# One TensorE visit for the values of a head pair's three tiles, in a fused windowed attention and feed-forward kernel

## The chip, the cores and the metric

The kernel runs on one core of one Trainium2 chip. The metric is the device time of one execution in microseconds. Engines are named as in the profile: PE is TensorE's matmul stream and PEld its weight loads, DVE is VectorE, ACT is ScalarE, POOL is GpSimd, SP is the engine that issues the DMAs (SPq its queue).

## The reference

Attention over 4 batches of 8 heads, 768 positions and 64 columns a head, in which a position sees the 4 first keys (sinks) and the last 128; its output, 3072 tokens of 512 columns, goes through a feed-forward of width 2048 with an ELU.

```python
scores = scale * np.matmul(q, k.transpose(0, 1, 3, 2))
rel = pos[:, None] - pos[None, :]
keep = (pos[None, :] < n_sink) | ((rel >= 0) & (rel < window))
scores = np.where(keep, scores, -1000000000.0)
a = np.exp(scores - np.max(scores, axis=-1, keepdims=True))
a = a / (np.sum(a, axis=-1, keepdims=True) + 1e-09)
x = np.matmul(a, v)   # then (B, S, H * D), as 3072 tokens of 512
h = x @ w_in
g = np.where(h > 0.0, h, np.exp(np.minimum(h, 0.0)) - 1.0)
out = g @ w_out
```

## The kernel before

The 3072 tokens are 24 tiles of 128, six to a batch, grouped into nine chunks (`SIZES`, L42): chunks 0 to 2 have two tiles, chunks 3 to 8 three. Each chunk goes through attention, head pair by head pair (four pairs of two heads), and then through the feed-forward, in 16 blocks of 128 hidden columns. The feed-forward of chunks 0 and 1 is cut in halves (`PARTS`), since the weights arrive and are converted meanwhile.

For a tile of a head pair, attention is a chain over all engines. TensorE makes the scores of the two heads (L560 and L561 for each head; L567 in the first two chunks) into two score banks. DVE masks them and takes the maximum (L586), ACT takes the exponential (L588), ACT and DVE make the reciprocal of the sum (L592, L593), ACT and DVE write the probabilities in a high and a low fp16 half into a buffer pq (L600, L601), POOL writes the sinks (L607 to L611), and SP issues a transposing DMA from pq to a buffer pt (L619). Then TensorE multiplies pt with the values (`values`, L622 to L635): 6 matmuls for the first tile of a batch, 12 for the second, 14 for the others. These three parts of po (one PSUM bank, `po=1` in `RINGS`) become the pair's x by ACT L643 and DVE L644. Keys come in as kqs and are split into a high part (ACT L503) and a low part (POOL L507, L509).

In the feed-forward an h block is 12 matmuls of a block's input weights with the x of the four pairs (`stage1`, L671); two h banks take turns. ACT L679, DVE L681 and L682 and ACT L684 with POOL L685 make the ELU in two halves; an acc block (`stage2`, L692) multiplies these with the output weights into one bank for each tile. A weight's conversion is ACT L287, DVE L288, L289 and L290, ACT L436, POOL L437, 32 times, all of it within the start-up.

The order on every engine is decided ahead of time by a planner (`Plan`, L94). Each step is a task with an engine, a cost in us, and the tasks that it needs. TensorE's tasks carry a place `pos`; they form lines (1 scores, 2 values, 0 the rest) whose own order is fixed by it. `forward` goes through the tasks as if they ran, and takes on TensorE the line head that is ready and has the earliest place; the other engines take the ready task with the earliest due time. It does this in 8 rounds and keeps the best. `keep_order` (L774) then emits the instructions in that order. A task on TensorE is emitted in one piece; waits are set for each instruction by the buffers that it reads and writes.

Before, each tile's values are a task of their own (L637), with a place that is the same for the tiles of a pair but for 0.01 a tile.

Of the kernel before, what the change touches and what calls it, by code (L numbers as in the profile page):

```python
# [44 lines left out]
PARTS = [(0, 0, HALF), (1, 0, HALF), (0, HALF, NF), (1, HALF, NF)] + [(c, 0, NF) for c in range(2, len(SIZES))]  # L45
LAG = 2
ROUNDS = 8
WHOLE = 2
DUP = 2
AHEAD = 5  # L50
V_AT = 7
V_AT0 = 5.0
# [41 lines left out]
class Plan:  # L94
# [7 lines left out]
    def add(self, eng, dur, fn, *args, deps=(), lat=0.0, pos=None, or_=None, line=0):  # L102

        t = Task(eng, dur, fn, args, deps, lat, pos)
        t.line = line
        if or_:
            t.ways[or_[0]] = or_[1:]
        self.tasks.append(t)
        return t

    def ring(self, name, writers, users):

        r = self.rings.setdefault(name, [])
        r.append((writers, users))
# [229 lines left out]
def fast_path(tc, ctx, first, kq, vx, wt, out, nw, flag):  # L344
# [44 lines left out]
    add, ring = plan.add, plan.ring  # L389
# [54 lines left out]
    base, pos = {}, 0  # L444
# [27 lines left out]
    def attention(c):  # L472
        ts = CHUNKS[c]
        nt, kts = len(ts), key_tiles(ts)
# [5 lines left out]
        if c == 0:  # L480
            at = [-3.0 - V_AT0 - 3.0 + 1.2 * (k - n) for k in range(n)]
        elif c == 1:
            at = [-1.0 + k * (base[c] - 1.0 - V_AT) / (n - 1) for k in range(n)]
        else:
            at = [base[c] - 2.0 - V_AT - (n - 1 - k) * (base[c] - base[c - 1]) / n for k in range(n)]
# [32 lines left out]
        k = 0  # L518
        for p in range(NP):
# [10 lines left out]
            va = add("ACT", act_us(vw, True), lambda vraw=vraw, vhi=vhi: nc.scalar.activation(vhi, vraw, AF.Copy, scale=V_SCALE), deps=[ld])  # L530
            vb = add("DVE", dve_us(vw) + 0.1, lambda vraw=vraw, vhi=vhi, vlo=vlo: nc.vector.scalar_tensor_tensor(vlo, vraw, V_SCALE, vhi, ALU.mult, ALU.subtract), deps=[va])
            v_users = []
            ring("vs", [ld or va], [va, vb])
            if far:

                vb = add("ACT", 0.3, lambda vhi=vhi, vlo=vlo: nc.scalar.activation(vhi[64:72, nk * P :], vlo[64:72, nk * P :], AF.Copy), deps=[vb])
            ring("vhl", [va], v_users)

            po = po_ps[slot("po")]
            vals = []  # L540
            for g in ts:
                t, j = g % NT, ts.index(g)
                nb = 1 if t == 0 else 2
# [90 lines left out]
                            vo = nk * P + e * D  # L634
                            nc.tensor.matmul(po[e * D : (e + 1) * D, oc], vhi[:, vo : vo + D], pt[:, 8, :], start=False, stop=end)  # L635

                val = add("PE", 0.17 * nb + (0.05 if t >= 2 else 0.0) + (0.2 if j == 0 else 0.0), values, deps=[tr, va, vb], pos=at[k - j + nt - 1] + (V_AT0 if c == 0 else V_AT) + 0.01 * j, line=2)  # L637
                ring("pt", [tr], [val])
                vals.append(val)
                v_users.append(val)  # L640
                k += 1
            xh, xl = x_room(qc)
            fa = add("ACT", act_us(qc, True), lambda xh=xh, po=po: nc.scalar.activation(xh, po[:, :qc], AF.Copy, scale=PO_SCALE), deps=[vals[-1]])  # L643
            fb = add("DVE", dve_us(qc) + 0.1, lambda xh=xh, xl=xl, po=po: nc.vector.scalar_tensor_tensor(xl, po[:, :qc], PO_SCALE, xh, ALU.mult, ALU.subtract), deps=[fa])  # L644
# [372 lines left out]
```

## Time and profile before

| | us |
|---|---|
| runs | 657.74, 660.30, 660.76 (median 660.3) |
| the profiled execution | 658.03 |
| its span, first to last instruction | 656.2 |
| busy: TensorE, DVE, ACT, POOL | 611.0, 458.4, 456.3, 338.8 |

The profile is of one execution. A line of its tables names the source line, the engine, the operation, and what is written from what. Busy times are sums over an engine's instructions with overlaps counted once, so the durations of an engine's rows can add up to more. Ends of matmuls are modelled: durations of neighbouring PE rows overlap, and what a block takes is read from start to start.

### The profile page before, as it was taken

How to read it: one execution, taken by the hardware profiler on the slowest of the kernel's cores; microseconds unless marked ns; L12 is line 12 of the kernel's file. 1: busy time of each engine (PE TensorE's matmuls, PEld its weight loads, DVE VectorE, ACT ScalarE, POOL GpSimd, SP SyncE). 2: the span in 40 equal slices, each digit the busy share in tenths (PEclk: the TensorE clock that was granted, in tenths of full speed). 3: DMA queues.
4: the chain of work that ended last, by engine and by line, in shares of the span. 5: the costliest groups of instructions: out<-in, count | busy, mean ns of one | idle time of the engine just before them, and what ended most of it. 6: DMA issues, size and time to landing. Idle time of an engine off the chain costs nothing.

```text
span 656.2 us, 13438 instructions
## 1 busy us (share of the span) xinstructions
PE 611.0 (93%) x4449; PEld 370.1 (56%) x4449; DVE 458.4 (70%) x1251; ACT 456.3 (70%) x1340; POOL 338.8 (52%) x497
## 2 busy tenths in 40 slices
PE   3678699789999999999999999999999999999995
PEld 2444466457777665655555565565555556555552
DVE  6999999987677757757676877757686786533222
ACT  4988798887788878767677877766677776523221
POOL 0156878785565767544446656544446654212221
PEclk9998699999999999999999999999999999999998
DMA  7898976765647556445454666454655733211001
GB/s 266 202 284 231 267 213 209 246 171 154 140 126 155 159 151 129 117 116 158 100 147 114 186 135 164 79 157 136 125 140 122 213 91 90 61 42 44 1 0 54
DMA packets 130110, 93.41 MB, mean 142 GB/s; under 512 B 104432, under 2 KB 109552, under 8 KB 130032
## 3 DMA queue, kind: packets, MB, share of 16 engines
q1 hardware_dynamic: 130032, 92.47, 53.2%
q8 instruction: 37, 0.61, 0.4%
q14 instruction: 41, 0.34, 0.2%
HBM read 59.94 MB, written 7.34 MB: 103 GB/s over the span
## 4 chain that ended last, share of the span: by engine, by line
PE 81%; DVE 8%; DMA 3%; ACT 2%; issue 2%; POOL 2%; SPq 0%; DVEq 0%; POOLq 0%; ACTq 0%
PE h L671 35%; PE acc L692 34%; PE po L630 5%; PE s L560 3%; PE s L561 3%; DMA pt<-pq 2%; DVE wv L290 2%; DVE wu L288 1%; DVE pq L601 1%; PE s L567 1%; DVE wu L289 1%; DVE g L681 1%; POOL w L437 1%; ACT e L588 1%; ACT pq L600 1%
## 5 line engine op out<-in xcount | busy, mean ns | idle before, releaser
L671 PE MATMUL h<-x,w 128*128 128x384 f16 (+1 forms) x1728 | 278.1, 312 | 6.1 <-DVE g L682 6.1
L685 POOL TENSOR_TENSOR gl<-g,gh 128x384 f16<-128x384 f32 (+1 forms) x144 | 125.7, 874 | 195.8 <-ACT gh L684 163.2
L671 PEld LDWEIGHTS <-w 128*128 128x128 f16 x1728 | 166.5, 99 | 100.6 <-POOL w L437 4.0
L692 PE MATMUL acc<-w,gh 128*128 128x512 f16 x768 | 194.2, 382 | 0.7 <-ACT gh L684 0.7
L681 DVE TENSOR_SCALAR g<-g 128x384 f32<-128x384 f32 (+1 forms) x144 | 68.2, 474 | 109.1 <-ACT g L679 108.8
L679 ACT ACTIVATE g<-h 128x384 f32<-128x384 f32 (+1 forms) x144 | 65.0, 451 | 84.6 <-PE h L671 77.3
L601 DVE SCALAR_TENSOR_TENSOR pq<-e,st,pq 128x256 f16<-128x256 f32 (+1 forms) x192 | 104.7, 573 | 15.1 <-ACT pq L600 14.5
L692 PE MATMUL acc<-w,gl 128*128 128x512 f16 x384 | 109.3, 380 | 2.4 <-POOL gl L685 2.3
L692 PEld LDWEIGHTS <-gh 128*128 128x128 f16 x768 | 70.0, 98 | 70.9 <-ACT gh L684 1.2
L586 DVE CUSTOM_DVE_ANT_0 e<-s,m 128x264 f32<-128x264 f32 (+1 forms) x192 | 73.5, 404 | 41.5 <-PE s L561 38.0
L588 ACT ACTIVATE e<-e,st 128x264 f32<-128x264 f32 (+1 forms) x192 | 93.4, 487 | 11.5 <-DVE st L586 10.1
L684 ACT ACTIVATE gh<-g 128x384 f16<-128x384 f32 (+1 forms) x144 | 69.2, 481 | 44.6 <-DVE g L682 44.1
L600 ACT ACTIVATE pq<-e,st 128x256 f16<-128x256 f32 (+1 forms) x192 | 84.6, 479 | 10.0 <-DVE st L593 9.4
L507 POOL TENSOR_TENSOR kq<-kqs,kq 128x396 fp32r<-128x396 f32 (+1 forms) x56 | 68.5, 1224 | 37.8 <-ACT kq L503 37.2
L682 DVE SCALAR_TENSOR_TENSOR g<-g,h 128x384 f32<-128x384 f32 (+1 forms) x144 | 72.5, 503 | 1.3
L692 PEld LDWEIGHTS <-gl 128*128 128x128 f16 x384 | 37.5, 98 | 49.0 <-POOL gl L685 4.1
L503 ACT ACTIVATE kq<-kqs 128x780 fp32r<-128x780 f32 (+2 forms) x56 | 48.5, 878 | 17.1 <-PE s L561 15.5
L509 POOL TENSOR_TENSOR kq<-kqs,kq 64x384 fp32r<-64x384 f32 (+1 forms) x56 | 57.0, 1017 | 4.4
L560 PE MATMUL s<-kq 128*128 128x264 f32 x160 | 56.0, 367 | 3.0 <-DVE st L586 2.1
L437 POOL TENSOR_TENSOR w<-wv,w 128x512 f16<-128x512 f32 x32 | 38.8, 1218 | 37.2 <-DVE wu L289 16.6
L630 PE MATMUL po<-pt,vh 128*64 128x128 f16 x704 | 42.1, 230 | 7.7 <-DVE x L644 5.0
L561 PE MATMUL s<-kq 128*128 128x264 f32 x160 | 42.8, 284 | 0.0
(78 smaller groups left out, 620.7 us busy)
## 6 DMA issues: line engine op xcount, KB each, us to landing
raw<-in_wt_dram SPq DMA_DIRECT2D x32, 512.0 KB, 5.2
kqs<-in_kq_dram SPq DMA_DIRECT2D x24, 456.0 KB, 3.4
kqs<-in_kq_dram SPq DMA_DIRECT2D x24, 390.0 KB, 3.3
out_dram<-wv SPq DMA_DIRECT2D x24, 256.0 KB, 2.4
vs<-in_vx_dram SPq DMA_DIRECT2D x20, 256.0 KB, 2.8
vm<-in_vx_dram SPq DMA_DIRECT2D x6, 768.0 KB, 4.8
kqs<-in_kq_dram SPq DMA_DIRECT2D x12, 326.0 KB, 3.4
vs<-in_vx_dram SPq DMA_DIRECT2D x12, 320.0 KB, 3.1
```

The source lines that it names most:

```text
L560: nc.tensor.matmul(sp[:, :wd], q, hi[:, c0 : c0 + wd], start=True, stop=False)
L586: red = add("DVE", 0.13 + 0.00145 * wd, lambda ee=ee, me=me, sp=sps[e], m=m, wd=wd: nc.vector.tensor_tensor_reduce(ee, sp[:, :wd], m[:, :w ...
L588: ex = add("ACT", 0.48 + 0.00085 * wd, lambda ee=ee, me=me, rs=rs[:, e : e + 1]: nc.scalar.activation(ee, ee, AF.Exp, bias=me, scale=-1.0, ...
L600: a = add("ACT", act_us(nb * P, True), lambda src=src, hi=hi, re=re: nc.scalar.activation(hi, src, AF.Copy, scale=re), deps=[rr])
L601: b = add("DVE", dve_us(nb * P) + 0.1, lambda src=src, hi=hi, lo=lo, re=re: nc.vector.scalar_tensor_tensor(lo, src, re, hi, ALU.mult, ALU. ...
L630: nc.tensor.matmul(po[e * D : (e + 1) * D, oc], vv[:, vo : vo + D], pt[:, (2 * e + part) * nb + i, :], start=new, stop=last)
L671: nc.tensor.matmul(hp[:, :n], win[:, part, d, :], xx[:, :n], start=k == 0, stop=k == 3 * ND - 1)
L681: b = add("DVE", 0.1 + 0.0008 * n, lambda gf=gf: nc.vector.tensor_scalar(gf, gf, -1.0, G_SCALE, ALU.add, ALU.mult), deps=[a])
L682: b = add("DVE", dve_us(n), lambda gf=gf, hp=hp: nc.vector.scalar_tensor_tensor(gf, gf, 0.0, hp[:, :n], ALU.min, ALU.max), deps=[b])
L684: th = add("ACT", act_us(n), lambda gf=gf, gh=gh: nc.scalar.activation(gh[:, :n], gf, AF.Copy), deps=[b])
L685: tl = add("POOL", pool_us(n), lambda gl=gl, gf=gf, gh=gh: nc.gpsimd.tensor_tensor(gl[:, :n], gf, gh[:, :n], ALU.subtract), deps=[th])
L692: nc.tensor.matmul(acc[i], gg[:, i * P : (i + 1) * P], wout[:, part, :], start=f == f0 and k == 0, stop=f == f1 - 1 and k == 2)
```

## The change

In a chunk of three tiles the three tiles' values become one task: it needs all three transposed blocks, is emitted in one piece, tile by tile, and frees their three pt buffers. In chunks of two tiles the tiles stay tasks of their own. The costs that the planner gives to values change for all chunks: 0.161 us a key tile in place of 0.17, 0.053 for the sinks, and 0.19 for each visit.

```diff
--- before.py
+++ after.py
@@ -45,6 +45,7 @@
 PARTS = [(0, 0, HALF), (1, 0, HALF), (0, HALF, NF), (1, HALF, NF)] + [(c, 0, NF) for c in range(2, len(SIZES))]
 LAG = 2
 ROUNDS = 8
+VISIT = 3
 WHOLE = 2
 DUP = 2
 AHEAD = 5
@@ -537,7 +538,7 @@
             ring("vhl", [va], v_users)
 
             po = po_ps[slot("po")]
-            vals = []
+            vals, visit = [], []
             for g in ts:
                 t, j = g % NT, ts.index(g)
                 nb = 1 if t == 0 else 2
@@ -634,11 +635,28 @@
                             vo = nk * P + e * D
                             nc.tensor.matmul(po[e * D : (e + 1) * D, oc], vhi[:, vo : vo + D], pt[:, 8, :], start=False, stop=end)
 
-                val = add("PE", 0.17 * nb + (0.05 if t >= 2 else 0.0) + (0.2 if j == 0 else 0.0), values, deps=[tr, va, vb], pos=at[k - j + nt - 1] + (V_AT0 if c == 0 else V_AT) + 0.01 * j, line=2)
-                ring("pt", [tr], [val])
+                dur = 0.161 * nb + (0.053 if t >= 2 else 0.0)
+                if nt < VISIT:
+                    val = add("PE", dur + 0.19 + (0.2 if j == 0 else 0.0), values, deps=[tr, va, vb], pos=at[k - j + nt - 1] + (V_AT0 if c == 0 else V_AT) + 0.01 * j, line=2)
+                    ring("pt", [tr], [val])
+                    vals.append(val)
+                    v_users.append(val)
+                else:
+                    users = []
+                    ring("pt", [tr], users)
+                    visit.append((values, dur, tr, users))
+                k += 1
+            if visit:
+
+                def together(visit=visit):
+                    for f, *_ in visit:
+                        f()
+
+                val = add("PE", sum(v[1] for v in visit) + 0.19, together, deps=[*(v[2] for v in visit), va, vb], pos=at[k - 1] + V_AT, line=2)
+                for v in visit:
+                    v[3].append(val)
                 vals.append(val)
                 v_users.append(val)
-                k += 1
             xh, xl = x_room(qc)
             fa = add("ACT", act_us(qc, True), lambda xh=xh, po=po: nc.scalar.activation(xh, po[:, :qc], AF.Copy, scale=PO_SCALE), deps=[vals[-1]])
             fb = add("DVE", dve_us(qc) + 0.1, lambda xh=xh, xl=xl, po=po: nc.vector.scalar_tensor_tensor(xl, po[:, :qc], PO_SCALE, xh, ALU.mult, ALU.subtract), deps=[fa])
```

The instructions are the same, in number and kind. On TensorE, in chunk 3's fourth pair, this is what stands at the second tile's values before. In these rows `s` are scores, `h` an h block, `po` values, and `pt_107` and `pt_108` the second and third tile's transposed block:

```order
L671 LDWEIGHTS w_162
L671 MATMUL h_165<-x,w_162 128x256
L560 MATMUL s_166<-kq_84 128x264
L561 MATMUL s_166<-kq_84 128x264
L630 LDWEIGHTS vh_87
L630 MATMUL po_168<-pt_107,vh_87 64x128
L630 LDWEIGHTS vh_87
L630 MATMUL po_168<-pt_107,vh_87 64x128
```

An h block and a score stand ahead of the second tile's values; its first tile's stand ahead of that h block. Now, at the end of the second tile:

```order
L631 LDWEIGHTS vh_87
L631 MATMUL po_168<-pt_107,vh_87 64x128
L631 LDWEIGHTS vh_87
L631 MATMUL po_168<-pt_107,vh_87 64x128
L631 LDWEIGHTS vh_87
L631 MATMUL po_168<-pt_108,vh_87 64x128
L631 LDWEIGHTS vh_87
L631 MATMUL po_168<-pt_108,vh_87 64x128
```

The third tile's values follow the second's with nothing between, as the second's do the first's. In the first chunks more moves, on all engines, since the planner's costs are others there. On DVE, the rows at the last weight's conversion (`wv_123` from `acc` and `wu_125`) before:

```order
L289 TENSOR_SCALAR wu_125<-raw_127 128x512
L288 TENSOR_SCALAR wu_125<-raw_127 128x512
L681 TENSOR_SCALAR g_109<-g_109 128x256
L531 SCALAR_TENSOR_TENSOR vl_88<-vs_72,vh_86 128x512
L682 SCALAR_TENSOR_TENSOR g_109<-g_109,h_164 128x256
L593 RECIPROCAL st_96<-st_96 128x2
L593 RECIPROCAL st_97<-st_97 128x2
L644 SCALAR_TENSOR_TENSOR x<-po_168,x 128x256
L290 SCALAR_TENSOR_TENSOR wv_123<-acc_171,wu_125 128x512
```

and in the new order (L290 is now L291, L289 is L290, L288 is L289, L681 and L682 are L699 and L700, L601 is L602, L531 is L532):

```order
L290 TENSOR_SCALAR wu_125<-raw_127 128x512
L699 TENSOR_SCALAR g_109<-g_109 128x256
L602 SCALAR_TENSOR_TENSOR pq_102<-e_93,st_96,pq_102 128x256
L700 SCALAR_TENSOR_TENSOR g_109<-g_109,h_164 128x256
L602 SCALAR_TENSOR_TENSOR pq_102<-e_93,st_96,pq_102 128x256
L289 TENSOR_SCALAR wu_125<-raw_127 128x512
L532 SCALAR_TENSOR_TENSOR vl_88<-vs_72,vh_86 128x512
L699 TENSOR_SCALAR g_110<-g_110 128x256
L291 SCALAR_TENSOR_TENSOR wv_123<-acc_171,wu_125 128x512
```

Two of the softmax's rows (`pq`) now stand between the parts of the conversion, and x (L644) has moved behind it. Counted in the two orders: up to the L682 of block 15 of chunk 0 there are two L601, one L593 and one L644 fewer than before; up to this last L290 there are two L601, one L681 and one L586 (with its read-out) more, and one L593 and one L644 fewer; up to the L682 of block 7 of chunk 0 there are five L586 more and no other difference, and up to that of block 9 two L601 and one L593 fewer and one L644 more. On POOL, at the last weight's low part (`w_163`) before, where `kq_85` and `kq_83` are the first two key splits of chunk 3:

```order
L437 TENSOR_TENSOR w_163<-wv_123,w_163 128x512
L507 TENSOR_TENSOR kq_85<-kqs_70,kq_85 128x396
L509 TENSOR_TENSOR kq_85<-kqs_70,kq_85 64x384
L685 TENSOR_TENSOR gl_116<-g_110,gh_113 128x256
L685 TENSOR_TENSOR gl_114<-g_109,gh_111 128x256
L507 TENSOR_TENSOR kq_83<-kqs_71,kq_83 128x396
L509 TENSOR_TENSOR kq_83<-kqs_71,kq_83 64x384
```

and in the new order (L437 is now L438, L507 and L509 are L508 and L510, L685 is L703):

```order
L510 TENSOR_TENSOR kq_85<-kqs_70,kq_85 64x384
L703 TENSOR_TENSOR gl_116<-g_109,gh_113 128x256
L438 TENSOR_TENSOR w_162<-wv_122,w_162 128x512
L703 TENSOR_TENSOR gl_114<-g_110,gh_111 128x256
L438 TENSOR_TENSOR w_161<-wv_121,w_161 128x512
L608 TENSOR_TENSOR st_96<-e_93,st_96 128x8
L611 CAST pq_102<-st_96 128x2x8
L612 TENSOR_TENSOR pq_102<-st_96,pq_102 128x8
L703 TENSOR_TENSOR gl_115<-g_109,gh_112 128x256
L508 TENSOR_TENSOR kq_83<-kqs_71,kq_83 128x396
L510 TENSOR_TENSOR kq_83<-kqs_71,kq_83 64x384
L438 TENSOR_TENSOR w_163<-wv_123,w_163 128x512
```

Both splits have moved ahead of `w_163`; the first one, of which the second row opens this piece, stands ahead of `w_162` and `w_161` too.

## Rows read from the trace of the kernel before

**Rows 1.** The page: the span, and the busy time of PE with its share and its number of instructions.

```profile
span 656.2 us, 13438 instructions
...
PE 611.0 (93%) x4449; PEld 370.1 (56%) x4449; DVE 458.4 (70%) x1251; ACT 456.3 (70%) x1340; POOL 338.8 (52%) x497
```

**Rows 2.** Stretches of time: from and to, length, then busy us and instructions of PE, PEld, DVE, ACT and POOL, the granted clock of TensorE, the share of DMA and its GB/s.

```profile
0.00:20.00 20.00, 7.41 (x30) 4.45 (x30) 14.03 (x66) 11.65 (x39) 2.50 (x18) 1.00 0.74 250
...
20.00:140.00 120.00, 96.45 (x738) 62.92 (x736) 115.60 (x276) 101.59 (x290) 81.23 (x108) 0.93 0.81 229
140.00:160.00 20.00, 18.49 (x149) 12.73 (x148) 15.26 (x43) 16.18 (x53) 14.92 (x24) 1.00 0.76 207
147.56:620.00 472.44, 472.44 (x3479) 284.44 (x3478) 313.69 (x865) 328.24 (x971) 241.88 (x356) 1.00 0.49 123
```

**Rows 3.** The table of waits of TensorE: who waited for whom, us in total, how many times, the longest.

```profile
PE s L567 <- DVE st L586: 9.6, 7, 3.7
...
PE h L671 <- DVE g L682: 6.1, 5, 2.2
PE po L630 <- DVE x L644: 5.0, 4, 2.0
...
PE po L630 <- DMA pt<-pq: 1.5, 3, 0.6
```

**Rows 4.** The timeline of TensorE: start, us, line and tiles, number of instructions. An h block, the values of chunk 3's third pair in one piece, and the acc block behind them.

```profile
200.26 1.47 PE L671 MATMUL h<-x,w 128*128 128x256 f16 x12
201.67 0.25 PE L630 MATMUL po<-pt,vh 128*64 128x128 f16 x2
...
202.75 1.04 PE L692 MATMUL acc<-w,gh 128*128 128x512 f16 x4
```

**Rows 5.** The same view: an h block with an acc block behind it.

```profile
147.56 1.47 PE L671 MATMUL h<-x,w 128*128 128x256 f16 x12
148.87 1.03 PE L692 MATMUL acc<-w,gh 128*128 128x512 f16 x4
```

**Rows 6.** The same view: the values of chunk 3's fourth pair in three visits, the first row of each and the row behind each.

```profile
213.49 0.25 PE L630 MATMUL po<-pt,vh 128*64 128x128 f16 x2
...
213.78 1.48 PE L671 MATMUL h<-x,w 128*128 128x256 f16 x12
...
215.43 0.30 PE L630 MATMUL po<-pt,vh 128*64 128x128 f16 x4
...
215.88 0.39 PE L560 MATMUL s<-kq 128*128 128x264 f32 x1
...
216.64 0.30 PE L630 MATMUL po<-pt,vh 128*64 128x128 f16 x4
...
217.16 1.04 PE L692 MATMUL acc<-w,gh 128*128 128x512 f16 x4
```

**Rows 7.** Groups of instructions by line and shape: busy us, mean ns of one, idle time before them. The two steps that make a pair's x in a chunk of three tiles.

```profile
L643 ACT ACTIVATE x<-po 128x384 f16<-128x384 f32 x24 | 11.6, 485 | 7.2 <-PE po L635 7.2
...
L644 DVE SCALAR_TENSOR_TENSOR x<-po,x 128x384 f16<-128x384 f32 x24 | 13.3, 553 | 2.2 <-ACT x L643 2.2
```

**Rows 8.** The timeline of TensorE: an h block of a three-tile chunk and the row behind it.

```profile
229.61 2.11 PE L671 MATMUL h<-x,w 128*128 128x384 f16 x12
231.65 0.30 PE L630 MATMUL po<-pt,vh 128*64 128x128 f16 x4
```

**Rows 9.** The timeline of TensorE: a late wait in the start-up.

```profile
127.87 1.47 PE L671 MATMUL h<-x,w 128*128 128x256 f16 x12 [1.46 <-DVE g L682]
```

**Rows 10.** Groups of DVE instructions by line and shape up to 145 us.

```profile
L601 DVE SCALAR_TENSOR_TENSOR pq<-e,st,pq 128x256 f16<-128x256 f32 x36 | 18.1, 545 | 0.2 <-ACT pq L600 0.2
L586 DVE CUSTOM_DVE_ANT_0 e<-s,m 128x264 f32<-128x264 f32 x40 | 16.0, 423 | 2.8 <-PE s L567 1.7 <-PE s L561 1.1
L681 DVE TENSOR_SCALAR g<-g 128x256 f32<-128x256 f32 x25 | 15.7, 626 | 1.1 <-ACT g L679 1.1
...
L644 DVE SCALAR_TENSOR_TENSOR x<-po,x 128x256 f16<-128x256 f32 x10 | 4.1, 411 | 0.1
```

**Rows 11.** Groups of POOL instructions by line and shape: the low parts of the keys.

```profile
L509 POOL TENSOR_TENSOR kq<-kqs,kq 64x384 fp32r<-64x384 f32 x48 | 49.7, 1034 | 3.8
...
L507 POOL TENSOR_TENSOR kq<-kqs,kq 128x396 fp32r<-128x396 f32 x32 | 35.8, 1117 | 17.0 <-ACT kq L503 16.6
```

**Rows 12.** Stretches of time again, of single lines: length, busy us and instructions. The first three rows are DVE's L289, the next two DVE's L681, the last two the whole of POOL.

```profile
0.00:40.00 40.00, 2.66 (x6) 1.00 0.83 254
40.00:120.00 80.00, 13.98 (x21) 0.89 0.84 232
120.00:145.00 25.00, 3.99 (x5) 1.00 0.63 193
...
40.00:120.00 80.00, 9.72 (x17) 0.89 0.84 232
120.00:145.00 25.00, 4.92 (x7) 1.00 0.63 193
...
40.00:120.00 80.00, 58.06 (x82) 0.89 0.84 232
120.00:145.00 25.00, 22.03 (x26) 1.00 0.63 193
```

## The prediction

> **What bounds the kernel now.** I read the views in this order. The page first: TensorE is busy 611.0 of 656.2 us, so it stands idle 45.2 us in all [rows 1]. The stretches tell where. Up to 20 us it is busy 7.41 us, from 20 to 140 us 96.45 of 120, from 140 to 160 us 18.49 of 20, which leaves it idle 12.6 + 23.6 + 1.5 = 37.7 us; from 147.56 to 620 us it is busy 472.44 of 472.44 us [rows 2]. (The rest of the 45 us lies behind 620, where the program ends.) So there are two regimes: a start-up of about 147 us, and a body in which nothing counts but TensorE's own instructions.
>
> In the start-up VectorE (DVE) is busy 115.60 of the 120 us from 20 to 140, against 101.59 of ScalarE (ACT), 96.45 of TensorE and 81.23 of GpSimd (POOL) [rows 2]. The table of waits agrees: TensorE's longest waits are for DVE rows, L586 (a score bank freed, 9.6 us), L682 (an h bank freed, 6.1) and L644 (the po bank freed, 5.0), while transposed blocks kept it waiting for 1.5 us in all, three times [rows 3]. The start-up is DVE's, the body TensorE's.
>
> **What the change does to the body.** The words of the change promise one visit in place of three, 48 visit heads fewer in 24 head pairs. But the planner already put a pair's tiles at one place, and in the order before 22 of the 24 pairs stand in one piece, such as the one that ran at 201.67 us [rows 4]. Only in chunk 3 is the first pair split into two visits and the fourth into three (it is the one in [rows 6]). From block 10 of chunk 3 on TensorE's order is the same, row for row. So three merges are left of 48.
>
> What is one worth? Whole, the values take 1.08 us (201.67 to the next acc block at 202.75), and the h block ahead of them takes 1.41 (200.26 to 201.67 [rows 4]) where an h block with acc behind it takes 1.31 (147.56 to 148.87 [rows 5]): a head of 0.10, 1.18 with it. Split in three, the values take 0.29, 0.45 and 0.52 (213.49 to 213.78, 215.43 to 215.88, 216.64 to 217.16 [rows 6]), 1.26 in sum and 1.56 with three heads. Two merges give 1.56 - 1.18 = 0.38, one 0.19. Three merges: **-0.6 us**, bounds 0 (if what is saved between visits comes back at the next switch) and 3 x 0.29 = 0.9 (the whole of the shortest visit each time).
>
> Joining adds a wait on paper: the planner lets the visit stand only where all three transposes are ready. On the chip the matmuls are issued by the same three calls in the same order and each keeps its own wait, so behind a late block only that block's matmuls and what follows them on TensorE stand, as before. In the body TensorE never waited, and the longest wait for a transposed block was 0.6 us [rows 2, 3]; I take 0, bound 4 pairs x 0.6 = 2.4. One neighbour comes closer: the fourth pair of chunk 3 now stands right ahead of that chunk's first h block, where an acc block lay between. That h block needs the pair's x, which ACT L643 (0.485) and then DVE L644 (0.553) make, 1.04 together [rows 7]. But it needs them only at its tenth and its twelfth matmul, and twelve take 2.04 (229.61 to 231.65), 0.17 each [rows 8]: the first nine, 1.53, cover ACT, eleven, 1.87, cover both. I take 0; with the cover gone it costs 1.04, once.
>
> **What the change does to the start-up.** The new planner costs (0.19 for each visit, in two-tile chunks too) reorder every engine there, and this is the larger unknown. Where DVE sets the pace, what matters is how much DVE work stands ahead of the rows that TensorE waits for late, such as the L682 that freed an h bank at 127.87 us [rows 9]. Up to the L682 of block 15 of chunk 0, the last block of that chunk, the new order has two L601 and one L644 fewer: 2 x 0.545 + 0.411 = 1.5 us sooner [rows 10]. Up to the last weight conversion (L290) it has two L601, one L681 and one L586 more and one L644 fewer: 1.090 + 0.626 + 0.423 - 0.411 = 1.7 us later (rows under 0.16 us are left out of both). TensorE's late waits are not for weights, so the former counts more. I take **-1.0**, bounds -1.5 and +1.7. Midway, at block 7 of chunk 0, the new order is later by five score rows (2.1 us), because it does scores ahead; it has made that up by block 9.
>
> POOL works the other way. Two key splits of chunk 3 (L507 and L509, 1.117 and 1.034 us [rows 11]) now stand ahead of the last weight's L437. A busy POOL goes with slow DVE rows: L289 takes 2.66 / 6 = 0.443 up to 40 us and 3.99 / 5 = 0.798 from 120 to 145, where POOL is busy 22.03 of 25 [rows 12]. Four POOL rows that each lengthen one DVE row by 0.355 make 1.4; I take **+0.5**, nearer to 0, since POOL is already busy 58.06 of the 80 us from 40 to 120 [rows 12] and other POOL rows move back in exchange.
>
> The Trainium skill ("SBUF — State Buffer", Who interferes with whom) says that GpSimd and a VectorE instruction in a 2-port mode take a shared pair of ports by turns, and that the loser blocks for the whole instruction of the other. The trace agrees in direction (0.443 against 0.798). By that rule the price would be up to the four rows' whole length, 2 x (1.117 + 1.034) = 4.3 in place of 0.5, and the sum below +2.7 in place of -1.1.
>
> **Sum.** -0.6 - 1.0 + 0.5 = -1.1. The profiled execution took 658.03 us (span 656.2 and 1.83 around it); one like it would take 656.9. The three runs shown lie at 657.74, 660.30 and 660.76 (median 660.3); the profiled one is among the short ones, and the mean of the four is 659.2. I forecast 659.2 - 1.1 = **658.1 us**.
>
> **Rivals.**
> A, the start-up gets tight. TensorE's early waits for the po bank and for score banks [rows 3] would come from an order that took visits for too cheap. If the honest costs remove DVE's slack, 120 - 115.60 = 4.4, and what TensorE idles from 140 to 160, 1.5, the gain is 4.4 + 1.5 + 0.6 = 6.5: 652.7. Against it: with DVE busy for 96% of the time no order gains more than that, and hardly one gains all of it.
> B, slower: POOL slows DVE. The new order gives POOL the key splits of chunk 2 earlier too, five ahead of weight 15 where three stood. If that makes the DVE rows from 40 to 120 us as slow as those from 120 to 145, L289 costs 21 x (0.798 - 0.666) = 2.8 and L681 17 x (0.703 - 0.572) = 2.2 more [rows 12]; 5.0 - 0.6 = +4.4, 663.6. It decides when POOL's busy share from 40 to 120 us rises from 73% to the 88% of the later stretch. Two early splits are 4.3 us, 5% of 80, so it should get a third of the way.
> C, the change does all that it says: 48 heads at 0.19, 9.1 us, 650.1. For it speak only the words; against it the 22 pairs that are whole already.
>
> **Chances.** Forecast 0.62, A 0.21, B 0.13, C 0.04. A measurement of this kernel can tell about 0.5%, 3.3 us, from no change. Faster by more than that takes C, most of A and a little of the forecast: 0.24. Slower takes most of B: 0.12. Within: 0.64. The three terms' bounds, all at one end, make the forecast's own range 656.8 (-0.9 - 1.5) to 662.3 (+1.7 + 1.4). The range 653 to 663 reaches into A and B and leaves out C, the far end of A and half of B, under 0.2.
>
> **What would show it.** In the changed profile TensorE is busy without a gap from about 146 us on; the fourth pair of chunk 3 is one visit of 1.1 us, and no wait stands in that chunk's first h block. TensorE's idle time up to 160 us is 35 to 39 us with DVE still busy for over 95% of 20 to 140 us. L289 near 0.67 from 40 to 120 us says that POOL did no harm, near 0.8 that B holds; an idle time near 32 us says A. I am wrong if TensorE waits in the body, or if the body is shorter by several us.

## The result, and the profile after

| | runs | median us | range | profiled execution | its span |
|---|---|---|---|---|---|
| before | 7 | 658.18 | 656.35 to 660.76 | 658.03 | 656.2 |
| after | 7 | 661.75 | 660.93 to 662.51 | 662.34 | 660.6 |

The changed kernel is slower: ratio 1.0057, 95% interval 1.0040 to 1.0074. The forecast was 658.1 us, a small gain. Two stretches of both traces place the 4.4 us by which the spans differ. The page of after, and its stretches and waits (columns as in [rows 2] and [rows 3]; source lines have moved: what was L567, L601, L619, L630, L644, L671, L682 and L692 is now L568, L602, L620, L631, L662, L689, L700 and L710):

```profile
span 660.6 us, 13426 instructions
...
PE 614.0 (93%) x4449; PEld 371.4 (56%) x4449; DVE 462.7 (70%) x1251; ACT 454.5 (69%) x1340; POOL 336.3 (51%) x497
```

```profile
20.00:140.00 120.00, 93.45 (x697) 59.58 (x695) 110.64 (x264) 97.53 (x280) 77.68 (x104) 0.92 0.82 229
140.00:160.00 20.00, 20.00 (x153) 13.50 (x151) 16.32 (x45) 15.61 (x52) 16.02 (x26) 0.95 0.78 171
151.97:620.00 468.03, 467.63 (x3467) 282.35 (x3466) 317.82 (x866) 326.38 (x968) 239.15 (x354) 1.00 0.51 125
```

```profile
PE po L631 <- DMA pt<-pq: 8.9, 7, 1.9
PE s L568 <- DVE st L587: 7.4, 10, 2.6
...
PE h L689 <- DVE g L700: 6.6, 3, 4.5
PE h L689 <- POOL w L438: 6.1, 5, 2.3
```

The h block that began at 147.56 us before [rows 5] begins at 151.97, 4.4 us later, so the whole loss is made in the start-up. DVE, its pacer, is busy 110.64 us from 20 to 140 us where it was 115.60 [rows 2]. TensorE's wait for transposed blocks (pt<-pq), 1.5 us in all before [rows 3], is 8.9. In the body TensorE is without a gap but for 0.40 us.

Up to the first 128x384 h block, that of chunk 3, both kernels have done the same 1434 matmuls (columns as in [rows 2]; before, then after):

```profile
0.00:218.46 218.46, 180.81 (x1434) 121.61 (x1435) 183.72 (x518) 177.05 (x537) 132.34 (x195) 0.96 0.74 203
```

```profile
0.00:223.33 223.33, 183.78 (x1434) 122.95 (x1435) 187.38 (x518) 175.62 (x536) 131.13 (x197) 0.95 0.75 199
```

Of the 4.9 us between the two, TensorE's idle time makes only 1.9 (39.55 against 37.65): the waits for transposed blocks grew by 7.4 us, but others went, such as that for x (5.0 us before). The other 3.0 us are the same matmuls taking longer. The mean granted clock is 0.95 against 0.96; no run changes the clock alone, so how much of this is the clock is not shown.

How far back does it go? The first h block of all began at 34.58 us before and begins at 39.37 now: 4.8 us, already there before 40 us. TensorE is busy 18.16 of the 34.58 us and 20.39 of the 39.37, so 2.6 us of it are idle time and 2.2 are work, with four more score matmuls ahead of the h block. The first rows below are the timeline of after (start, us, engine, line, tiles; in brackets the idle time ahead of a row and what ended it; SPq is the queue in which SP issues its DMAs), the second those of before. They show the values of head pair 3 of chunk 0, on which that block waits.

```profile
30.17 0.33 SPq L497 DMA_DIRECT2D kqs<-in_kq_dram  x1
...
30.61 0.37 SPq L528 DMA_DIRECT2D vs<-in_vx_dram  x1
...
31.04 1.19 SPq L620 DMA_TRANSPOSE pt<-pq  x1
...
32.28 0.58 SPq L416 DMA_DIRECT2D raw<-in_wt_dram  x1
...
32.96 1.80 SPq L620 DMA_TRANSPOSE pt<-pq  x1
...
36.49 0.32 PE L631 MATMUL po<-pt,vh 128*64 128x128 f16 x2 [1.69 <-DMA pt<-pq]
...
38.58 0.42 PE L631 MATMUL po<-pt,vh 128*64 128x128 f16 x4 [1.56 <-DMA pt<-pq]
...
39.37 1.03 PE L689 MATMUL h<-x,w 128*128 128x256 f16 x4
```

```profile
28.26 2.56 SPq L619 DMA_TRANSPOSE pt<-pq  x2
...
30.87 0.57 SPq L415 DMA_DIRECT2D raw<-in_wt_dram  x1
...
32.30 0.32 PE L630 MATMUL po<-pt,vh 128*64 128x128 f16 x2 [0.38 <-DMA pt<-pq]
...
34.58 4.35 PE L671 MATMUL h<-x,w 128*128 128x256 f16 x24
```

Before, both transposes of the pair go out together at 28.26 us and the chunk's next key, value and weight loads follow. After, SP has the key load (L497) and the value load (L528) of chunk 1 first and a weight load (L416) between the two. SP's own waits in after from 24 to 32 us:

```profile
SPq L497 <- PE s L568: 4.0, 2, 2.9
SPq L620 <- DVE pq L602: 2.3, 2, 1.2
```

The key load waits up to 2.9 us for the scores that still read its buffer, and nothing behind it on SP goes meanwhile. The Trainium skill ("DMA: Bandwidth & Descriptors", Anatomy of one DMA — SWDGE (gpsimd) path) says that the wait for a semaphore happens on the issuing sequencer, not in the DMA engines; these rows agree, 2.9 us. The pair's transposes lost little by it, though: the key load went out at 30.17 us, and the pair's last probabilities (pq) come from DVE only at 31.0 and 32.1 us, where they were done by 28.76 before (DVE in after, then in before):

```profile
30.01 1.00 DVE L602 SCALAR_TENSOR_TENSOR pq<-e,st,pq 128x128 f16<-128x128 f32 x3
...
31.63 0.48 DVE L602 SCALAR_TENSOR_TENSOR pq<-e,st,pq 128x256 f16<-128x256 f32 x1
```

```profile
27.36 1.40 DVE L601 SCALAR_TENSOR_TENSOR pq<-e,st,pq 128x256 f16<-128x256 f32 x4
```

DVE's waits between 20 and 45 us, in after (before's longest one there is 0.8 us):

```profile
DVE x L662 <- ACT x L661: 3.8, 2, 2.2
```

DVE stands 1.65 us at 27.29 and 2.18 us at 39.89 ahead of the x rows of pairs 1 and 3, whose values wait for their blocks. For pair 1 SP is not the reason: its second transpose goes out at 21.32 us in both kernels and lands 4.5 us later before, 4.6 after. TensorE takes these values sooner in after, ahead of scores that stood first (27.03 us before), and waits for the block:

```profile
25.98 0.42 PE L631 MATMUL po<-pt,vh 128*64 128x128 f16 x4 [1.86 <-DMA pt<-pq]
```

### The profile page after: what moved, and what is told of

It is laid out like the page before. It is cut to its first block, busy times and chain, and to the rows that moved or that the text cites. A ratio compares the mean times of both kernels' runs of the same rounds, so it can differ in the third digit from the quotient of the medians.

```text
span 660.6 us, 13426 instructions
## 1 busy us (share of the span) xinstructions
PE 614.0 (93%) x4449; PEld 371.4 (56%) x4449; DVE 462.7 (70%) x1251; ACT 454.5 (69%) x1340; POOL 336.3 (51%) x497
## 4 chain that ended last, share of the span: by engine, by line
PE 77%; DVE 7%; ACT 5%; DMA 4%; issue 4%; POOL 2%; SPq 0%; POOLq 0%; ACTq 0%; DVEq 0%
PE h L689 33%; PE acc L710 33%; PE po L631 4%; DMA pt<-pq 3%; PE s L561 3%; PE s L562 3%; DVE wv L291 1%; PE s L568 1%; ACT pq L601 1%; DVE pq L602 1%; DVE wu L289 1%; DVE g L699 1%; DMA kqs<-in_kq_dram 1%; ACT e L589 1%; ACT g L697 1%
## 5 line engine op out<-in xcount | busy, mean ns | idle before, releaser
L689 PE MATMUL h<-x,w 128*128 128x384 f16 (+1 forms) x1728 | 280.4, 313 | 14.3 <-DVE g L700 6.6
L703 POOL TENSOR_TENSOR gl<-g,gh 128x384 f16<-128x384 f32 (+1 forms) x144 | 126.6, 880 | 212.6 <-ACT gh L702 166.9
L689 PEld LDWEIGHTS <-w 128*128 128x128 f16 x1728 | 166.7, 99 | 109.6 <-POOL w L438 8.0
L710 PE MATMUL acc<-w,gh 128*128 128x512 f16 x768 | 195.0, 384 | 0.0
L699 DVE TENSOR_SCALAR g<-g 128x384 f32<-128x384 f32 (+1 forms) x144 | 69.9, 486 | 108.4 <-ACT g L697 108.0
L602 DVE SCALAR_TENSOR_TENSOR pq<-e,st,pq 128x256 f16<-128x256 f32 (+1 forms) x192 | 111.5, 608 | 17.3 <-ACT pq L601 16.6
L710 PE MATMUL acc<-w,gl 128*128 128x512 f16 x384 | 110.0, 382 | 1.3 <-POOL gl L703 1.3
L710 PEld LDWEIGHTS <-gh 128*128 128x128 f16 x768 | 71.1, 99 | 70.2 <-issue 1.7
L601 ACT ACTIVATE pq<-e,st 128x256 f16<-128x256 f32 (+1 forms) x192 | 84.5, 479 | 11.5 <-DVE st L594 11.1
L508 POOL TENSOR_TENSOR kq<-kqs,kq 128x396 fp32r<-128x396 f32 (+1 forms) x56 | 67.0, 1197 | 26.0 <-ACT kq L504 25.4
L700 DVE SCALAR_TENSOR_TENSOR g<-g,h 128x384 f32<-128x384 f32 (+1 forms) x144 | 72.6, 504 | 1.4
L710 PEld LDWEIGHTS <-gl 128*128 128x128 f16 x384 | 37.6, 98 | 48.3 <-POOL gl L703 2.8
L438 POOL TENSOR_TENSOR w<-wv,w 128x512 f16<-128x512 f32 x32 | 39.4, 1239 | 43.7 <-ACT w L437 23.6
L510 POOL TENSOR_TENSOR kq<-kqs,kq 64x384 fp32r<-64x384 f32 (+1 forms) x56 | 56.3, 1005 | 4.4
L631 PE MATMUL po<-pt,vh 128*64 128x128 f16 x704 | 41.3, 228 | 8.9 <-DMA pt<-pq 8.9
```

The source lines that it names most:

```text
L601: a = add("ACT", act_us(nb * P, True), lambda src=src, hi=hi, re=re: nc.scalar.activation(hi, src, AF.Copy, scale=re), deps=[rr])
L602: b = add("DVE", dve_us(nb * P) + 0.1, lambda src=src, hi=hi, lo=lo, re=re: nc.vector.scalar_tensor_tensor(lo, src, re, hi, ALU.mult, ALU. ...
L689: nc.tensor.matmul(hp[:, :n], win[:, part, d, :], xx[:, :n], start=k == 0, stop=k == 3 * ND - 1)
L699: b = add("DVE", 0.1 + 0.0008 * n, lambda gf=gf: nc.vector.tensor_scalar(gf, gf, -1.0, G_SCALE, ALU.add, ALU.mult), deps=[a])
L700: b = add("DVE", dve_us(n), lambda gf=gf, hp=hp: nc.vector.scalar_tensor_tensor(gf, gf, 0.0, hp[:, :n], ALU.min, ALU.max), deps=[b])
L703: tl = add("POOL", pool_us(n), lambda gl=gl, gf=gf, gh=gh: nc.gpsimd.tensor_tensor(gl[:, :n], gf, gh[:, :n], ALU.subtract), deps=[th])
```

## The experiments

Each ratio is to the kernel before in the same session. "First h" is the start of the first h block, "first wide h" that of the first 128x384 h block (chunk 3), both from the one profiled execution; between two executions of one order the latter can move by over 1 us (joined and joined_but_last have one order up to 210 us).

| kernel | us | ratio to before, 95% interval | first h | first wide h |
|---|---|---|---|---|
| before | | 1 | 34.58 | 218.46 |
| after | 661.75 | 1.0057 (1.0040 to 1.0074) | 39.37 | 223.33 |
| joined | 658.95 | 1.0023 (1.0005 to 1.0041) | 34.55 | 218.41 |
| joined_but_last | 658.03 | 1.0008 (0.9991 to 1.0025) | 34.62 | 216.93 |
| start_of_after | 661.58 | 1.0066 (1.0042 to 1.0090) | 39.16 | 222.89 |
| start_of_before | 659.70 | 1.0018 (1.0002 to 1.0035) | 34.49 | 220.09 |
| x_rows_later | 664.14 | 1.0089 (1.0074 to 1.0104) | 40.53 | 226.36 |
| pq_rows_first | 665.58 | 1.0109 (1.0089 to 1.0129) | 41.88 | 225.52 |
| transposes_first | 660.09 | 1.0028 (1.0013 to 1.0042) | 36.71 | 221.86 |
| both_first | 663.05 | 1.0070 (1.0048 to 1.0091) | 37.23 | 223.06 |
| loads_first_in_before | 666.10 | 1.0127 (1.0101 to 1.0153) | 41.28 | 225.39 |
| all_transposes_first | 660.62 | 1.0041 (1.0026 to 1.0057) | 36.28 | 221.36 |
| all_first | 660.62 | 1.0039 (1.0025 to 1.0052) | 35.98 | 221.74 |
| scores_first | 660.13 | 1.0024 (1.0012 to 1.0037) | 35.47 | 221.89 |
| back_rule | 660.26 | 1.0043 (1.0028 to 1.0058) | 34.34 | 221.29 |
| before_rule | 661.44 | 1.0059 (1.0046 to 1.0072) | 35.76 | 222.39 |
| jbl_rule | 662.05 | 1.0074 (1.0057 to 1.0091) | 35.85 | 223.14 |
| lat24 | 662.45 | 1.0081 (1.0063 to 1.0099) | 42.58 | 223.40 |
| g_rows_earlier | 661.47 | 1.0049 (1.0030 to 1.0068) | 39.03 | 222.47 |
| start_and_g_rows | 660.34 | 1.0018 (0.9997 to 1.0039) | 33.81 | 220.59 |

**The joining alone, and the start-up alone.** In joined the planner is that of before; behind it, the three value tasks of a pair in a three-tile chunk are emitted at the place of the last. In start_of_after and start_of_before the tasks up to the first h block are taken in the other kernel's order (a table of their numbers, FRONT), the rest in the kernel's own. The first diff is that of joined, the second that of the other two.

```diff
+    for row in pairs:
+        fns = [t.fn for t in row]
+        for t in row[:-1]:
+            t.fn = lambda: None
+        row[-1].fn = lambda fns=fns: [f() for f in fns]
     keep_order(tc, tasks)
```

```diff
+    first_ = [next(t for t in tasks if t.n == n) for n in FRONT]
+    rest = set(FRONT)
+    tasks = first_ + [t for t in tasks if t.n not in rest]
```

> The whole order of the kernel before, with the values of a head pair's three tiles moved to the place of the last of them. Theory S (the loss lies in the order that the planner writes for the start-up, and the joining in chunk 3 is worth its three visits): 658.2 - 3 x 0.19 = 657.6 us, ratio 0.998 to 1.000, first h block near 34.6 us as before. Rival J (joining costs by itself, through a longer visit or a wait for the last transposed blocks): 660 to 662, with waits of TensorE for pt<-pq behind 160 us.

> The kernel before, without any joining, but its first tasks, up to the first h block, stand in the order of the kernel after; everything later keeps the order before. Theory S: the 4.8 us by which the first h block came later come back here, 661.5 to 663.5 us, first h block at 38.5 to 39.5 us. Rival L (the order between 40 and 146 us makes the loss, and the first 40 us are caught up): at most 659.5. Rival J: 658.2, as before.

> The kernel after, but its first tasks, up to the first h block, stand in the order of the kernel before. Theory S: 661.75 - 4.4 = 657.3 us (656.5 to 658.5), first h block near 34.6 us. Rival L: 661 to 662.5, since the order from 40 us on is that of after. Rival J: 661 to 662.

start_of_after has nothing joined and is as slow as after: the order of the first 40 us holds the loss. start_of_before takes back most of it, though 0.18% is left. joined is not faster, as Theory S had it, but neither does it lose what rival J asked: 658.95 is 0.5 us above the before of its session (658.41), not 2 to 4, and the waits for pt<-pq behind 160 us did not come. Its interval leaves out 1 by 0.05%, of which the profiled execution shows nothing (span 656.1 us). The split of the 4.9 us into idle and busy time shows in these traces too: up to the wide h block TensorE is idle 38.7 and 38.3 us and busy 179.7 and 178.6 in joined and joined_but_last, which keep before's order in the start-up, but idle 39.1 and busy 183.8 in start_of_after. The trace of joined shows where the gain of the merges went. The first pair of chunk 3 gives 0.20 us: the lead over before is 0.18 us at the h block of 173.91 (174.09 before) and 0.38 at that of 178.25 (178.63). In the fourth pair, split in three before [rows 6], the timeline of joined has this:

```profile
211.66 1.04 PE L694 MATMUL acc<-w,gh 128*128 128x512 f16 x4
...
215.66 0.39 PE L560 MATMUL s<-kq 128*128 128x264 f32 x1 [0.73 <-DVE st L586]
...
216.09 0.25 PE L630 MATMUL po<-pt,vh 128*64 128x128 f16 x2
...
218.41 2.12 PE L673 MATMUL h<-x,w 128*128 128x384 f16 x12
```

The two visits that stood between scores before had covered DVE's e rows, which free the two score banks. With them gone TensorE waits 0.73 us. From the acc block to the wide h block takes 6.75 us here and took 6.37 before (212.09 to 218.46): the two merges cost 0.38 us net. In after the same place has a wait of 0.40. joined_but_last leaves this pair split:

```diff
-            if nt == 3:
+            if nt == 3 and (c, p) != (3, 3):
                 pairs.append(vals)
```

> As the run joined, but pair 3 of chunk 3 keeps its three visits. Reading of the run joined: each visit that goes is worth 0.2 us where TensorE has other work (lead over before 0.18 us at 150 us, 0.38 at 178 us), but in pair 3 the two visits had covered the wait for the score slots, and a wait of 0.73 us came in their place. So here the first 128x384 h block at 218.41 - 0.73 + 0.39 = 218.07 us, no wait for st in 214 to 217 us, and 0.3 us less than joined, too little to tell in the medians. If the wait of 0.73 us has another cause, it stays and the h block comes at 218.4 to 218.8 us.

The wait is gone and the stretch takes 6.39 us (210.54 to 216.93), as before. The wide h block came sooner than expected, by more than the merge: that part was made before 210 us, where this kernel and joined do not differ, and is spread between executions. The times of joined and joined_but_last cannot be told apart.

**Which rows of the start-up.** The next kernels are after, with a few tasks put ahead of another one in the order (n is the task, row what goes ahead of it):

```diff
+    for n, row in AHEAD_OF:
+        moved = [next(t for t in tasks if t.n == m) for m in row]
+        tasks = [t for t in tasks if t.n not in row]
+        i = next(i for i, t in enumerate(tasks) if t.n == n)
+        tasks[i:i] = moved
     keep_order(tc, tasks)
```

> The kernel after with TensorE's order as it is; only ScalarE's and VectorE's rows of the x values of head pairs 1 and 3 of chunk 0 (with the two e rows of the scores that TensorE does behind pair 1's values) stand a few rows later, behind work that is ready. Theory S in its narrow form (VectorE stands in its in-order queue for values that wait for late transposed blocks): the waits of 1.65 and 2.18 us at 27.29 and 39.89 us go, 661.75 - 3.8 = 658.0 us (657.2 to 659.5). Rival P (what costs is TensorE's own order, the scores of chunk 1 behind the waiting values; the rows on VectorE only show it): 661 to 662, the waits gone from x<-ACT but back at other rows.

> The kernel after, with ScalarE's and VectorE's rows that make the probabilities (pq) of head pair 3 of chunk 0 moved ahead of their rows for the x values of pair 1, as they stand in the kernel before; TensorE's and SP's orders untouched. Theory Q (the first h block is paced by pair 3's transposed blocks, which are late for two reasons together: their pq rows stand behind pair 1's x, and on SP their issue stands behind the key load L497 that waits for the scores S1.0.3): the rows alone bring little, since SP still holds the issue until 30 to 31 us: 660.5 to 662.5 us, first h block 38 to 40 us. Rival R (the rows' order on VectorE is enough): 657 to 659, first h block near 35 us.

> The kernel after, with SP's two transposes of pair 3 of chunk 0 ahead of the key load, the value load and the weight load that stand before and between them; all other orders untouched. Theory Q: pq is ready at 31.0 and 32.1 us only, so the issues come at 31.0 and 32.3 in place of 31.04 and 32.96: 0.7 us at most, 661 us (660.3 to 662), first h block 38.5 to 39.4 us. Rival T (SP's order is enough): 657 to 659, first h block near 35 us.

> Both moves at once on the kernel after: pair 3's pq rows ahead of pair 1's x rows, and its two transposes ahead of the loads on SP; TensorE's order is that of after. Theory Q: pq ready near 28.8 us, issues at about 28.3 us and 29.6 us, first values of pair 3 near 32.5 us, first h block 34.5 to 36 us, 657.8 us (657 to 659). Rival P (TensorE's own order, scores of chunk 1 behind waiting values, makes the loss): 661 to 662.5.

The narrow form of my theory fell: x_rows_later is slower than after, 1.0089 against 1.0057, as rival P had it or worse. The wait at DVE's x fell to 0.4 us, and others came in its place. These are DVE's waits between 20 and 45 us in x_rows_later:

```profile
DVE g L700 <- ACT g L698: 2.0, 1, 2.0
DVE st L595 <- ACT st L594: 1.9, 1, 1.9
```

ACT now had pair 3's vh row (L532) ahead, and that needs the buffer that pair 1's values hold, which wait for the same transposed blocks (it waited 0.98 us for them at 27.08 us). pq_rows_first and both_first met the like: ACT's pq rows at 29.08 and 29.04 us had waited 2.1 and 2.3 us for a pq buffer that pair 2's transpose had not yet read; so theory Q's sum of two causes fell too (both_first 1.0070, not 1.000). Moving the key, the value and the weight load on SP behind the two transposes, with no compute row touched, gave back half: transposes_first is 1.0028, and its first h block came 2.7 us sooner, not 0.7. The expectation counted issue times only, and the two go out no sooner (from 31.18 us on, against 31.04 and 32.96 in after). What changed is the landing: median 2.9 us from issue for the two, against 5.5 in after with the loads around them (SP's rows in transposes_first, then DMA issues between 28 and 34 us in transposes_first and in after; columns: count, median us to landing):

```profile
31.18 3.23 SPq L621 DMA_TRANSPOSE pt<-pq  x2
```

```profile
pt<-pq SPq DMA_TRANSPOSE x2, 2.9
```

```profile
pt<-pq SPq DMA_TRANSPOSE x2, 5.5
```

**SP's order in both directions.** loads_first_in_before puts into before what after has there, AHEAD_OF = [(334, [481, 447, 346, 50, 333])] (pair 3's values; key load, value load, transpose, weight load, transpose). By this edit one more weight load, which before issues behind the two transposes (30.87 us), goes ahead of them too, at 27.42 us. The other three go on from transposes_first.

> The kernel before with one thing of after: on SP the key load and the value load of chunk 1 (L496, L527) stand ahead of the two transposes of head pair 3 of chunk 0, and a weight load (L415) between the two. TensorE's, VectorE's and ScalarE's orders are those of before, nothing is joined. Theory SP (the start-up loses because SP, which issues in order, holds ready transposes behind loads that wait for a buffer): the key load waits for the scores S1.0.3, which end near 31.9 us, so the transposes are issued at 32 to 34 us in place of 28.26 us, the first h block comes at 38 to 39.5 us in place of 34.58, and the time is 660.5 to 662.5 us. Rival P (TensorE's and VectorE's orders make the loss): 658 to 659, since these are as before and VectorE has other work.

> As transposes_first, and also the transposes of pair 2 ahead of the key load and the value load that stand before them on SP; VectorE's order is that of after. Theory SP: pair 2's blocks land sooner, but its values wait for pair 1's x (32.15 us in the run before this), so little more than transposes_first: 659.3 to 660.5 us, first h block 36 to 37 us. If pair 2's place counts by itself: 658 to 659.

> As both_first, and also the transposes of pair 2 ahead of the key and value loads on SP, so that the pq slot for which ScalarE waited 2.31 us at 29.04 us in both_first is free sooner. Theory SP: with that wait gone pair 3's pq rows end near 28.8 us, the first h block comes at 34.5 to 36 us, 658 to 659.5 us. Rival P: 661 to 663, the wait turns up at another row.

> As transposes_first, and TensorE does the scores S1.0.2 ahead of pair 1's values, as in the kernel before, with VectorE's two e rows of these scores ahead of pair 1's x. Theory: the rest of the loss is the wait of 1.6 us of VectorE for pair 1's x at 27.8 us; two e rows (0.86 us) now fill it, so 0.8 to 1.6 us sooner than transposes_first: 658.5 to 659.5 us, first h block 35 to 36 us. If the rest lies behind 40 us instead: 660, as transposes_first.

The reverse test cost more than expected, 8 us, by this one wait of TensorE (waits between 18 and 45 us, loads_first_in_before):

```profile
PE po L631 <- DMA pt<-pq: 7.6, 1, 7.6
```

SP stood 3.5 us at the key load there, the transposes went out at 32.31 and 34.21 us, and VectorE, whose order is that of before, waited 7.3 us at pair 3's x. So SP's order alone is enough for such a loss, against rival P; that the orders of TensorE and VectorE add nothing in after is not shown by it. all_first and scores_first brought the first h block to 35.98 and 35.47 us, nearly to before's 34.58, but the time no further than transposes_first, 1.1 and 0.6 us above the ranges expected of them: from there on the kernels with the transposes first spend 185.1 to 186.4 us up to the wide h block, before 183.9 and after itself 184.0. In transposes_first this is not waiting (columns as in [rows 2]):

```profile
0.00:221.86 221.86, 184.48 (x1435) 123.45 (x1435) 189.80 (x518) 175.94 (x536) 130.70 (x197) 0.95 0.71 200
```

TensorE is idle for 37.4 us there, no more than before (37.7), and busy for 3.7 us longer with the same work. all_first (37.5 idle, 3.4 longer) and scores_first (37.8, 3.2) are alike, all_transposes_first (38.9, 1.6) lies between. In the first three the loss that stays is longer busy time; the mean granted clock is 0.95, 0.95 and 0.94 against 0.96 before, and whether it makes all of it is open.

**Is it a rule?** back_rule, before_rule and jbl_rule let SP issue a transpose ahead of the load before it wherever the planner has its pq ready by 1 us after that load (up to 146 us); lat24 is after with lat=2.4 in place of lat=1.0 in the transposing task (L620). The condition of the rule:

```diff
+        while t.line == 3 and k and sq[k - 1].line != 3 and max(d.start + d.dur for d in t.deps if d) < sq[k - 1].start + SLACK:
```

> As start_of_before, and behind it, up to 146 us, SP issues a transpose ahead of the load that stands directly before it wherever the planner's own times have its pq ready no later than 1 us after that load (six such swaps behind 40 us). Theory SP for the rest: TensorE's waits for pt<-pq between 45 and 146 us fall from 6.5 us to 4 us or less, and the time to 658.0 to 659 us. If the rest is not SP's: 659.3 to 660.5, as start_of_before, and the waits stay.

> The kernel before with the same rule on SP (six swaps, the first of them ahead of the value load of chunk 1 at 27.47 us). TensorE waits for pt<-pq little in before, so little can be had: 656.5 to 658.5 us, ratio 0.998 to 1.001. If loads that come later cost more than transposes that come sooner: 659 to 661.

> joined_but_last with the same rule on SP: both small gains together, 656.5 to 658.5 us, ratio 0.997 to 1.001; slower only if before_rule is slower.

> The kernel after with one number changed: the planner counts 2.4 us in place of 1.0 for the time a transpose takes behind its issue (the trace has 4.5 us from issue to landing in this stretch, the planner had some 3.3). Every engine's order in the start-up is written anew. By theory SP an order that still has the key load K1.4 ahead of pair 3's transposes (this one has) is late at the first h block, 37 to 40 us, 660 to 663 us. If the planner's landing time were the cause as such: 656 to 658.5.

It is not. before_rule and jbl_rule are slower than the kernels they start from by over 0.5%, and back_rule (1.0043 against 1.0018) and lat24 (1.0081 against 1.0057) are no faster. In back_rule TensorE's waits for pt<-pq between 45 and 146 us did fall, from 6.5 to 4.0 us, and the time did not follow. In before_rule the value load of chunk 1 went out at 29.51 us behind a transpose that itself waited for pq, where it had gone at 27.47; ACT's vh row came late, and TensorE waited for it, 1.6 us:

```profile
33.47 0.32 PE L631 MATMUL po<-pt,vh 128*64 128x128 f16 x2 [1.57 <-ACT vh L531]
```

So a ready load held behind a waiting transpose can make TensorE wait as a ready transpose behind a waiting load does; what this one of the six swaps costs of the 0.6% is not shown. lat24 agrees with Theory SP in time only: its first h block came at 42.58 us, outside the 37 to 40 expected, and up to 45 us TensorE waits there for no transposed block, but for score banks, 2.9 us at 41.05. Another new order lost as much in another way.

**The rest.** The last two move two ELU rows of DVE ahead of weight rows, AHEAD_OF = [(207, [642, 643])], on after and on start_of_before.

> The kernel after with two rows of VectorE moved: the ELU rows L699 and L700 of block 12 of chunk 0 stand ahead of the conversion rows of weight 29 (four conversion rows, some 3 us, sooner). Theory W (the rest of the loss is the one wait of 4.5 us at 137.55 us and the lower clock behind it): the wait shrinks to 1 to 2 us, the clock stays high, h there takes 1.5 us, 1 to 2.7 us sooner, 659 to 660.7 us. Rival D (VectorE has the same work in all, so what it does first only moves the wait): 661.3 to 662.5, with a wait of 2 us or more for weights (w L438) a few us later.

> start_of_before with the same two rows moved. Theory W: 659.7 less 1 to 2.7, 657 to 658.7 us, ratio 0.998 to 1.000, and the first 128x384 h block at 217.5 to 219.1 us. Rival D: 659 to 660.5.

The wait of 4.5 us became one of 2.5 for weight rows and one of 0.95 for POOL, and the granted clock fell as in after (0.83 from 130 to 140 us, 0.77 there; timeline of TensorE in g_rows_earlier):

```profile
135.44 0.28 PE L690 MATMUL h<-x,w 128*128 128x256 f16 x1 [2.52 <-DVE wu L291]
136.67 2.53 PE L690 MATMUL h<-x,w 128*128 128x256 f16 x11 [0.95 <-POOL w L439]
```

The times are within the intervals of after and start_of_before. Rival D holds, and what is left between start_of_before and before, 0.02 to 0.35%, stays open: it is no more than joined shows by itself.

## Why the prediction was wrong

- **Bounds.** Right: two regimes, and a body in which only TensorE's own instructions count. Right too that 22 of 24 pairs were whole already, so that rival C had nothing to give.
- **Three merges, -0.6 us.** A merge is worth 0.20 us (0.19 predicted) where other work fills TensorE. The bound of 0 at the other end was wrong: two of the three cost 0.38 net, since the visits had covered the wait for the score banks, so the three together gain nothing. The prediction asked which wait the joined visit would meet, not which wait the split ones hid.
- **Waits for transposed blocks, 0.** Right behind 160 us. It was priced only for the body and for the joined visits, with 1.5 us in all in the trace of before. In the start-up, where no visit is joined, they were put at nothing without a reason, and became 8.9 us. Their sum does not measure the loss, though: start_of_before still has 7.9 us of them.
- **DVE order in the start-up, -1.0 us, bounds -1.5 and +1.7.** This is the step that failed. It counted how many DVE rows stand ahead of the rows that TensorE waits for late, and so took DVE's idle time as given (4.4 us from 20 to 140 us); it became 9.4. DVE lost not by its row counts but by waiting for values whose transposed blocks came late: for pair 1 since TensorE took the values sooner (1.86 us), for pair 3 since three loads stood around its transposes on SP (5.5 us to landing in place of 2.9). The prediction looked at neither order in the first 40 us. In place of -1.0 the start-up took 4.4 us more; start_of_after shows that the first 40 us hold it, and transposes_first that about half is SP's three loads. The other half is not taken apart. The later weights, which the prediction set aside, are not it: after waits 6.1 us for them (POOL w L438), start_of_after not at all, at the same time.
- **POOL, +0.5 us, and rival B.** Not there. The group that was L289 takes 12.07 / 20 = 0.604 us from 40 to 120 us in after, where it took 0.666 [rows 12], with POOL busy 58.35 of 80 us as before. The price of 4.3 us by the port rule of the Trainium skill ("SBUF — State Buffer", Who interferes with whom) did not show either. B's figure of 663.6 was near the result by another cause.
- **Rival A.** Against it the prediction set DVE's busy share of 96%; it fell to 92%. A rival "the new order makes DVE wait" was missing. That the time lies in the stated range, and even in the forecast's own of 656.8 to 662.3, is luck: its upper end adds 1.7 us of DVE rows and 1.4 of POOL's hindrance, and neither is what happened.
- **What would show it.** One visit of 1.08 us in the fourth pair of chunk 3 and no wait in that chunk's first h block: right. TensorE idle 39.1 us up to 160 us: just past the 35 to 39 named, and only 1.5 more than before, so this sign missed most of the loss. DVE over 95% busy: wrong, and that was the row that told.

## What to carry to other kernels

When a change of costs lets a planner reorder a start-up, compare the order of the queue that issues the DMAs first: a load that waited for its buffer held two transposes behind it for 4 us (loads_first_in_before), and loads around two transposes went with 2.6 us more to their landing (after). None of this is in DVE's or TensorE's row counts. Read TensorE's busy time up to a fixed block beside its idle time, since a loss can pass from one to the other. Ask of each piece of work that is moved away what wait it covered where it stood. And apply an edit to the old order by hand before believing its time: here the edit alone gained nothing (joined 1.0023, joined_but_last 1.0008), and the reordered first 40 us alone cost 0.66% (start_of_after).

## What was not expected of the hardware

Two transposes landed 2.9 us after their issue with no load directly ahead of them and 5.5 us with a key, a value and a weight load issued around them (326, 256 and 512 KB). After a wait of 4.5 us at 137.55 us in after, TensorE's h block took 2.72 us in place of 1.47, at a granted clock of 0.50 from 137.55 to 140 us, the lower of its two levels (1.2 GHz): this wait was paid a second time in the matmuls behind it. The length of a wait alone does not decide that: behind one of 1.46 us in before [rows 9] the block took 1.47, and behind one of 1.45 in start_of_after, at 132.04 us, it took 2.72.
